# A transformer block on one core: V kept in DRAM as pairs of rows, and a newly searched order

## The chip, the core and the metric

The kernel runs on one core of a Trainium2 chip. A core has five engines that run their own instruction streams and meet through semaphores: PE (TensorE, the matrix multiplier), DVE (VectorE), ACT (ScalarE), POOL (GpSimd) and SP (SyncE), which here does nothing but issue transfers to the core's 16 DMA engines. The metric is device time in microseconds (us) for one execution; lower is better. The time before is the median of three runs, 244.95 us (243.38 to 245.19).

## What is computed

A block with adaptive layer norm on 2048 tokens of width 512: a dilated sliding-window attention with 32 heads of 16, then a gated feed-forward (FFN) of width 1792. Cut to what matters:

```python
mod = (silu(c) @ w_mod).reshape(...)          # sa, ca, ga, sb, cb, gb
h = layernorm(x) * (1 + ca) + sa
qkv = (h @ wqkv)                              # H = 32 heads, Dh = 16
W, dil = (8, 2)
idx = arange(S)[:, None] - arange(W)[None, :] * dil      # token s sees s, s-2, ..., s-14
logits = einsum('bhsd,bhswd->bhsw', q, k[idx]) * Dh ** -0.5    # idx < 0 is masked
o = einsum('bhsw,bhswd->bhsd', softmax(logits), v[idx])
x = x + ga * (o @ wo)
h = layernorm(x) * (1 + cb) + sb
x = x + gb * ((silu(h @ w1) * (h @ w3)) @ w2)
```

## The kernel before

The 2048 tokens are 16 tiles T of 128. Tensors are bfloat16; sums are kept in PSUM in float32, in 8 banks of 128 x 512.

**QKV.** Layer norm and projection run over four groups of four tiles. Q and K are kept transposed (channels on partitions). V is projected with tokens on partitions (`proj_v`, matmuls of L796), evicted by ACT (L806) into one of `NVB = 6` buffers `vb`, and stored to a DRAM scratch `v_dram`, one row of 512 channels (1 KB) per token, with 16 rows of zeros ahead of token 0 (written once from `zrow`). A buffer of `vb` is free again when its store has landed.

**Logits** (`logits`). For a tile, DVE multiplies q by the eight shifted views of k in one instruction (L827). PE sums over the 16 channels of each head by matmuls with the 0/1 matrix `E_sb` (L836): four column groups of the array run side by side, each for 32 of the tile's tokens. The result has 32 rows (heads) per group of 32 tokens; its columns are shift by token, the tokens in the order "even ones, then odd ones".

**Softmax** (`shift`, `exps`, `softmax`). DVE and ACT work on these columns, for two tiles at once; PE turns the result (L891), so that partitions are (token pair, shift) and the two tokens of a pair lie in the free dimension; ACT evicts it to `al` (L895).

**Values** (`values`). Four loads per tile, one for every 32 tokens, bring V from DRAM back to `vsh`: 128 pieces of 2 KB each. Partition (t, w) gets the two neighbouring rows 2t - 2w and 2t + 1 - 2w, so 16 pairs by 8 shifts. DVE multiplies by the weights in place (L911). PE sums over the eight shifts with a 0/1 matrix `ind` (L920), ACT evicts (L926) into `oa`, and a DMA transpose turns that into `ot`, which is multiplied by `wo` (L944) and added to x by DVE (L948). There are three `vsh` buffers (one of them in the place of `wqkv`, once the projections are done) and two `oa`.

**FFN.** Six groups of two or four tiles (`FFN`): PE computes gate and up (L960), ACT and DVE make silu(gate) * up, PE multiplies by w2 (L1003, L991), DVE adds x and the result is stored. The weights come in four column slices each, `w1_0` to `w1_3`, `w3_0` to `w3_3`.

**Order.** The builder first makes about 1200 operations with what each reads and writes. A list `ORDER`, found ahead of time by a search over a cost model, gives the sequence; every engine runs its operations in that sequence and none overtakes another on its engine. A list `SLOTS` gives the buffer of each value. `PACKET` and the cost constants were used by the search alone and do nothing in the kernel as it runs. On PE the FFN matmuls of the first tiles are placed between the attention work of later tiles. All transfers but one go through SP's queue, issued by L124: weights, V stores, V loads, transposes and output stores stand there in one line, and where one of them has to wait for a semaphore, those behind it wait too. The words "58th on SP" below count positions in this line from zero.

Of the kernel before, what the change touches and what calls it, by code (L numbers as in the profile page):

```python
# [256 lines left out]
def c_act(n):  # L257
    return 66 + n * 107 // 128
# [8 lines left out]
PACKET = {T: 95 if T < 2 else 122 for T in range(16)}  # L267
# [7 lines left out]
AVCOL = frozenset(range(16))  # L275
# [5 lines left out]
def _build(p, A_x, A_wqkv, A_wo, B_w1, B_w3, B_w2, c, w_mod, out):  # L281
# [34 lines left out]
    ind = sb([P, 2, 16, 2], bf, "ind")  # L316
    before = sb([P, W, 2, 16], bf, "before")
# [25 lines left out]
    zrow = at([PAD, D], bf, "zrow", 25600)  # L343
# [54 lines left out]
    p.op("pool", lambda e: e.memset(ind[:], 0.0), 100, k, w=[vind])  # L398
    for r in range(2):
        p.op("pool", lambda e, r=r: e.memset(ind[:, r, :, r], 1.0), 100, k, w=[vind])  # L400
    for edge, mult in ((0, 1), (W - 1, -1)):
        p.op("pool", lambda e, edge=edge, mult=mult: e.affine_select(
            out=ind[:], in_=ind[:], compare_op=ALU.is_ge, fill=0.0, base=edge, pattern=[[0, 2], [-W * mult, 16], [0, 2]],
            channel_multiplier=mult), 250, k, w=[vind])
    p.op("pool", lambda e: e.memset(before[:], 0.0), 250, k, w=[vbefore])
    p.op("pool", lambda e: e.affine_select(out=before[:], in_=before[:], compare_op=ALU.is_ge, fill=BEFORE, base=0,
                                           pattern=[[-DIL, W], [1, 2], [2, 16]], channel_multiplier=0), 400, k, w=[vbefore])
# [36 lines left out]
    p.dma(v_dram[0:PAD, :], zrow[:], ("load", 11), (16, 1024), r=[vzrow] + wm_hold, w=[vvpad], store=True)  # L444
# [345 lines left out]
    def proj_v(T, tt, vh):  # L790
# [19 lines left out]
        p.dma(v_dram[PAD + T * P:PAD + (T + 1) * P, :], lambda: vt.at[:], k, (128, 1024), r=[vt], w=[vd], cost=400, store=True)  # L810
# [5 lines left out]
    def logits(Ts):  # L816

        vl = Val("ps_l", psum)
        for i, T in enumerate(Ts):
# [10 lines left out]
            def red(e, i=i, T=T, vp=vp):  # L830
                c0 = vl.at * 512 + i * W * 32
                if T == 0:
                    e.matmul(PALL[0:32, c0:c0 + W * 32], ones[:, 0:32], before[:], start=True, stop=False, tile_position=(0, 0))
                for ft in range(KT):
                    for q in range(4):
                        ins = e.matmul(PALL[32 * q:32 * q + 32, c0:c0 + W * 32], E_sb[:, ft, :], bass.AP(vp.at, ft * P + 32 * q, [[W * KT * P, P], [KT * P, W], [1, 2], [2, 16]]),  # L836
                                       start=(ft == 0 and (T > 0 or q > 0)), stop=(ft == KT - 1), tile_position=(0, 32 * q))
                return ins

            p.op("pe", red, C_RED + (110 if T == 0 else 0), ("lg", T), r=[vp, vE] + ([vbefore, vc] if T == 0 else []), part=[vl], tiled=True)  # L840
# [32 lines left out]
    def softmax(Ts, vl, ve, vx_):  # L873
# [12 lines left out]
        def turn(e):  # L886
            b = bank(vt).bitcast(bf)
            for i in range(n):
                at = b[:, i * 256:(i + 1) * 256].rearrange("p (q y h) -> p q y h", q=4, y=2)
                for y in range(2):  # L890
                    ins = e.transpose(at[:, :, y, :], bass.AP(ve.at[0], i * W * 32 + y * 16 * W, [[2 * W * 32, P], [1, P]]), ident[:])  # L891
            return ins
# [6 lines left out]
    def values(T, i, val):  # L899
# [3 lines left out]
        for q in range(4):  # L903
# [11 lines left out]
        if T in AVCOL:  # L915
            def acc(e):
                b = bank(vo)
                for r in range(2):
                    for q in range(4):
# [4 lines left out]
            p.op("pe", acc, C_RED, ("ac", T), r=[vv, vind], w=[vo], tiled=True)  # L924
            va = Val("oa", oapool)
            p.op("act", lambda e: e.activation(va.at[:], bank(vo), ACT.Copy), c_act(512), ("ac", T), r=[vo], w=[va])  # L926
            p.dma(lambda: vt.at[:], lambda: va.at[:], ("ac", T), (128, 1024), r=[va], w=[vt], cost=1250, transpose=True)
        else:
            def acc(e):
                b = bank(vo)  # L930
                for g in range(4):
                    for ft in range(KT):
                        for r in range(2):
                            ins = e.matmul(b[:, ft * P + 32 * g:ft * P + 32 * g + 32], vv.at[:, 2 * g + r, ft * P:(ft + 1) * P],
                                           ind[:, r].rearrange("p t r -> p (t r)"), start=(r == 0), stop=(r == 1))
                return ins

            p.op("pe", acc, C_ACC, ("ac", T), r=[vv, vind], w=[vo])
            p.op("act", lambda e: e.activation(vt.at[:].rearrange("p k t -> p (k t)"), bank(vo), ACT.Copy), c_act(512), ("ac", T), r=[vo], w=[vt])
# [224 lines left out]
```

## Time and profile before

| | |
|---|---|
| median of 3 runs | 244.95 us |
| the profiled execution, its own time | 245.03 us |
| its span, first to last instruction | 243.0 us |
| instructions | 4593 |
| granted TensorE clock | 1.00 throughout |
| issues of V loads | 64, of 256 KB each |
| issues of V stores | 16, of 128 KB each |

The profile is of one execution. Busy times are per engine; a busy PE is not PE at its peak, since ends of matmuls are modelled. "PEld" is the loading of the stationary operand, which runs beside the matmuls. In views of waits, "A <- B" is an instruction A that sat idle until B released it; L124 is the line of the helper that issues every DMA, so DMAs are told apart by their tiles.

### The profile page before, as it was taken

The page shows a single profiled execution, that of the slowest core. Times are in us where ns is not written, and L with a number is a line of the kernel's source. Part 1 is how long each engine was busy: PE and PEld are TensorE (multiplying, and loading weights), DVE is VectorE, ACT ScalarE, POOL GpSimd, SP SyncE. Part 2 cuts the span into 40 slices and gives each one's busy share as a digit, 9 for nine tenths or more (in the row PEclk, how much of TensorE's full clock was granted, in tenths as well). Part 3 has the DMA queues.
Part 4 walks back from the last instruction along what each step waited for, and adds up shares of the span by engine and source line. Part 5 has one row for each costly group of instructions (what it writes and reads, how often), then busy time and mean ns, then how long its engine had stood idle before and what let it go on. Part 6 is the DMA issues. An engine that isn't in the chain of part 4 may idle for free.

```text
span 243.0 us, 4593 instructions
## 1 busy us (share of the span) xinstructions
PE 232.6 (96%) x1789; PEld 134.1 (55%) x1814; DVE 169.1 (70%) x295; ACT 158.3 (65%) x324; POOL 23.0 (9%) x54
## 2 busy tenths in 40 slices
PE   7899999999789999999999999999999999999995
PEld 1665454545357885654444444444655447576874
DVE  5489999999697999999999698366133213155242
ACT  4358597799788978777967798876653674321300
POOL 6421330011001100011000040110000100000000
DMA  5999899599589999699897824884020030011002
GB/s 167 288 361 265 272 298 215 134 272 275 175 196 291 256 242 245 154 214 137 251 227 195 237 65 68 194 182 99 3 65 1 3 86 0 0 46 43 3 23 65
DMA packets 44685, 38.33 MB, mean 158 GB/s; under 512 B 19560, under 2 KB 35960, under 8 KB 44664
## 3 DMA queue, kind: packets, MB, share of 16 engines
q1 hardware_dynamic: 44656, 38.04, 62.6%
q8 instruction: 14, 0.23, 0.4%
q14 instruction: 7, 0.06, 0.1%
q10 hardware_dynamic: 8, 0.00, 0.0%
HBM read 29.62 MB, written 4.21 MB: 139 GB/s over the span
## 4 chain that ended last, share of the span: by engine, by line
PE 65%; DMA 14%; SPq 7%; ACT 6%; DVE 5%; issue 2%; POOL 1%; ACTq 0%
PE pall L960 33%; PE pall L1003 14%; SPq L124 7%; PE pall L777 5%; DMA sb_wm_g<-in_w_mod_dram 4%; DMA sb_ot<-sb_oa 4%; PE pall L944 3%; DMA v_scratch_dram<-sb_v 3%; PE pall L991 3%; PE pall L796 2%; PE pall L920 2%; DMA sb_h<-sb_xn 2%; PE pall L836 2%; ACT sb_h L653 2%; ACT sb_xn L620 1%
## 5 line engine op out<-in xcount | busy, mean ns | idle before, releaser
L960 PE MATMUL pall<-sb_h,sb_w 128*128 128x256 bf16 (+1 forms) x668 | 103.0, 308 | 1.4 <-DMA sb_w<-in_B_w_dram 0.7
L960 PEld LDWEIGHTS pall<-sb_h,sb_w 128*128 128x128 bf16 x672 | 64.4, 98 | 38.0 <-ACT sb_hh L970 1.5
L966 ACT ACTIVATE sb_sg<-pall 128x256 bf16<-128x256 f32 (+1 forms) x84 | 35.0, 453 | 33.5 <-PE pall L960 25.9
L1003 PE MATMUL pall<-sb_w,sb_hh 128*128 128x512 bf16 x187 | 43.2, 379 | 0.6
L827 DVE TENSOR_TENSOR sb_pq<-sb_q,sb_kT 128x4096 bf16<-128x4096 bf16 x16 | 36.3, 2277 | 0.0
L970 ACT ACTIVATE sb_hh<-pall 128x256 bf16<-128x256 f32 (+1 forms) x56 | 26.5, 494 | 10.3 <-PE pall L960 10.3
L1003 PEld LDWEIGHTS pall<-sb_w,sb_hh 128*128 128x128 bf16 x196 | 18.9, 98 | 21.3 <-DVE sb_hh L971 0.6
L974 DVE TENSOR_TENSOR sb_hh<-sb_sg,pall 128x256 bf16<-128x256 bf16 x28 | 11.1, 418 | 26.6 <-PE pall L960 23.3
L911 DVE TENSOR_TENSOR sb_vsh<-sb_vsh,sb_al 128x4096 bf16<-128x4096 bf16 x12 | 27.4, 2286 | 2.4 <-ACT sb_al L895 1.3
L777 PE MATMUL pall<-sb_h,sb_wqkv 128*128 128x512 bf16 x107 | 25.8, 379 | 1.2 <-ACT sb_v L806 0.9
L971 DVE TENSOR_TENSOR sb_hh<-sb_sg,sb_hh 128x256 bf16<-128x256 bf16 (+1 forms) x56 | 17.9, 349 | 7.3 <-ACT sb_sg L966 4.0
L1019 DVE TENSOR_TENSOR sb_o<-pall,sb_x 128x512 bf16<-128x512 f32 (+1 forms) x18 | 11.0, 627 | 13.4 <-PE pall L1003 7.3
L626 POOL TENSOR_SCALAR sb_rs<-sb_var 128x2 f32<-128x2 f32 x8 | 4.9, 608 | 145.5 <-ACT sb_xn L620 145.5
L777 PEld LDWEIGHTS pall<-sb_h,sb_wqkv 128*128 128x128 bf16 x112 | 10.3, 98 | 12.0 <-ACT sb_v L806 1.4
L944 PE MATMUL pall<-sb_wo,sb_ot 128*128 128x512 bf16 x60 | 15.7, 379 | 0.9 <-DMA sb_ot<-sb_oa 0.5
L796 PE MATMUL pall<-sb_wqkv,sb_h 128*128 128x512 bf16 x61 | 15.9, 379 | 0.3 <-issue 0.2
L653 ACT ACTIVATE sb_h<-sb_h,sb_modc 128x512 bf16<-128x512 bf16 (+1 forms) x20 | 13.2, 721 | 3.9 <-DMA sb_h<-sb_xn 3.9
L948 DVE SCALAR_TENSOR_TENSOR sb_x<-pall,sb_x 128x512 bf16<-128x512 f32 x16 | 10.9, 688 | 6.5 <-PE pall L944 6.5
L631 ACT ACTIVATE sb_xn<-sb_x,sb_nb,sb_rs 128x512 bf16<-128x512 bf16 x16 | 12.6, 808 | 4.1 <-DVE sb_nb L628 4.1
L620 ACT ACTIVATE sb_xn<-sb_x,sb_nm 128x512 bf16<-128x512 bf16 x16 | 11.5, 720 | 2.9 <-DVE sb_nm L616 2.7
L785 ACT ACTIVATE sb_q<-pall 128x512 bf16<-128x512 f32 x16 | 9.3, 604 | 4.4 <-PE pall L777 4.4
L594 DVE BATCH_NORM_STATS2 sb_st<-sb_x 128x6 f32<-128x512 bf16 x15 | 9.9, 676 | 2.7 <-DMA sb_x<-in_A_x_dram 2.7
(112 smaller groups left out, 236.1 us busy)
## 6 DMA issues: line engine op xcount, KB each, us to landing
sb_vsh<-v_scratch_dram SPq DMA_DIRECT2D x48, 256.0 KB, 4.9
sb_vshx<-v_scratch_dram SPq DMA_DIRECT2D x16, 256.0 KB, 4.0
sb_w<-in_B_w_dram SPq DMA_DIRECT2D x6, 512.0 KB, 7.8
sb_w<-in_B_w_dram SPq DMA_DIRECT2D x6, 384.0 KB, 4.4
v_scratch_dram<-sb_v SPq DMA_DIRECT2D x16, 128.0 KB, 4.3
out_dram<-sb_o SPq DMA_DIRECT2D x14, 128.0 KB, 2.0
sb_x<-in_A_x_dram SPq DMA_DIRECT2D x3, 512.0 KB, 9.8
sb_wqkv<-in_A_wqkv_dram SPq DMA_DIRECT2D x2, 512.0 KB, 7.9
```

Of the source, the lines that this page charges most:

```text
L124: return e.dma_start(a, b, transpose=True) if transpose else e.dma_start(a, b)
L653: return e.activation(vh.at[:, ft, 0:n * P], vh.at[:, ft, 0:n * P], ACT.Identity, bias=modc[:, 8 * which + ft:8 * which + ft + 1], scale=m ...
L777: ins = e.matmul(bank(vp)[:, 0:n], wqkv[:, t, kind * D + ft * P:kind * D + (ft + 1) * P], vh.at[:, t, 0:n], start=(t == ORDER[0]), stop=(t ...
L796: ins = e.matmul(bank(vp), vh.at[:, t, tt * P:(tt + 1) * P], wqkv[:, t, 2 * D:3 * D], start=(t == ORDER[0]), stop=(t == ORDER[-1]))
L827: return e.tensor_tensor(vp.at[:], in0, in1, ALU.mult)
L911: return e.tensor_tensor(v_w, v_w, a_w, ALU.mult)
L944: ins = e.matmul(bank(vy), vt.at[:, ft, :], wo[:, ft, :], start=(ft == 0), stop=(ft == KT - 1))
L960: ins = e.matmul(bank(vp)[:, 0:n], wt[:, t, fi * P:(fi + 1) * P], vh.at[:, t, 0:n], start=(t == 0), stop=(t == KT - 1))
L966: p.op("act", lambda e: e.activation(vt.at[:, 0:n], bank(vgp)[:, 0:n], ACT.Silu), c_act(n), k, r=[vgp], w=[vt], table="silu")
L970: p.op("act", lambda e: e.activation(vh_.at[:, 0:n], bank(vup)[:, 0:n], ACT.Copy), c_act(n), k, r=[vup], w=[vh_])
L971: p.op("dve", lambda e: e.tensor_tensor(vh_.at[:, 0:n], vt.at[:, 0:n], vh_.at[:, 0:n], ALU.mult), 60 + n * 69 // 128, k, r=[vt], w=[vh_], ...
L1003: ins = e.matmul(bank(vz), vhh[fi].at[:, tt * P:(tt + 1) * P], w2[:, fi, :], start=(fi == 0), stop=(fi == NF - 1))
```

## The change

`v_dram` now has one row of 2 KB per token: its first half holds V two tokens back, its second half V of the token itself. Every V row is therefore written twice: the store of a tile has 256 pieces of 1 KB instead of 128, from the same SBUF tile read twice. The zeros ahead are 18 rows of 2 KB, and the store of tile 0 overlaps them, so it waits until the zeros have landed.

A load still has 128 pieces of 2 KB, but partition (t, w) is now one token t of 32 and one of four double shifts w: its piece holds the rows t - 4w - 2 and t - 4w. There are still four loads per tile and eight rows of 512 in each partition of `vsh`. The tokens of the logits stand in their own order, so L836 reads its moving operand contiguously instead of in steps of two; the turn of the weights (L891) takes shift by token with a step of two instead of contiguous columns; `ind` is one matrix of 128 x 32 for both halves instead of two. The branch for tiles outside `AVCOL`, which no tile took, goes, and a branch for tiles in `EARLY`, which is empty, comes. Two POOL instructions that built `ind` go.

`ORDER` and `SLOTS` are replaced. The operations are the same ones otherwise, so the two sequences can be compared. On PE the first 47 operations, up to the keys of the first tiles, are the same. Positions on SP of what the prediction speaks of, read from the two lists (V_T: store of tile T; L_T: loads of tile T; ot_T: transpose of tile T):

| | before | after |
|---|---|---|
| zeros | 21 | 18 |
| V0, V1 | 22, 23 | 22, 23 |
| wmg1 (last columns of w_mod) | 17 | 21 |
| w1_0, w3_0 | 61, 69 | 19, 59 |
| L0, L1 | 25 to 35 | 26 to 33 |
| V9, V8 | 58, 59 | 44, 61 |
| V5, V7 | 47, 50 | 58, 53 |
| L2, L3 | 44 to 57 | 45 to 55 |
| w1_1, w3_1 | 49, 60 | 56, 47 |
| first of L5 | 62 | 62 |
| ot_2, ot_3 | 63, 65 | 60, 64 |

Buffers of `vb`: before, V12 and V15 take the buffers of V9 and V8, and are evicted 76th and 81st on ACT. After, V15, V14 and V13 take those of V7, V5 and V8, and are evicted 85th, 84th and 89th. On PE the first FFN matmul stands at 157 in both; before it uses w1_1 and the next w3_1, w1_0, w1_2; after, the first eight use w1_1, w1_0 and w3_1 and w3_0.

```diff
+WL = 4
+TB = W // DIL
+EARLY = frozenset(())
...
-    ind = sb([P, 2, 16, 2], bf, "ind")
-    before = sb([P, W, 2, 16], bf, "before")
+    ind = sb([P, P // WL], bf, "ind")
...
-    v_dram = nc.dram_tensor("v_scratch_dram", (PAD + S, D), bf)
+    v_dram = nc.dram_tensor("v_scratch_dram", (PAD + S + DIL, 2 * D), bf)
...
-    p.dma(v_dram[0:PAD, :], zrow[:], ("load", 11), (16, 1024), r=[vzrow] + wm_hold, w=[vvpad], store=True)
+    p.dma(bass.AP(v_dram, 0, [[2 * D, PAD + DIL], [D, 2], [1, D]]), bass.AP(zrow, 0, [[D, PAD + DIL], [0, 2], [1, D]]), ("load", 11), (36, 1024), r=[vzrow] + wm_hold, w=[vvpad], store=True)
...
-        p.dma(v_dram[PAD + T * P:PAD + (T + 1) * P, :], lambda: vt.at[:], k, (128, 1024), r=[vt], w=[vd], cost=400, store=True)
+        p.dma(bass.AP(v_dram, (PAD + T * P) * 2 * D + D, [[2 * D, P], [3 * D, 2], [1, D]]), lambda: bass.AP(vt.at, 0, [[D, P], [0, 2], [1, D]]), k,
+              (256, 1024), r=[vt] + ([vvpad] if T == 0 else []), w=[vd], cost=400, store=True)
...
-                        ins = e.matmul(PALL[32 * q:32 * q + 32, c0:c0 + W * 32], E_sb[:, ft, :], bass.AP(vp.at, ft * P + 32 * q, [[W * KT * P, P], [KT * P, W], [1, 2], [2, 16]]),
-                                       start=(ft == 0 and (T > 0 or q > 0)), stop=(ft == KT - 1), tile_position=(0, 32 * q))
+                        cols = [q, [TB, 32]] if T in EARLY else [32 * q, [1, 32]]
+                        ins = e.matmul(PALL[32 * q:32 * q + 32, c0:c0 + W * 32], E_sb[:, ft, :],
+                                       bass.AP(vp.at, ft * P + cols[0], [[W * KT * P, P], [KT * P, W]] + cols[1:]),
+                                       start=(ft == 0 and (T > 0 or q >= NBEF)), stop=(ft == KT - 1), tile_position=(0, 32 * q))
...
-                    ins = e.transpose(at[:, :, y, :], bass.AP(ve.at[0], i * W * 32 + y * 16 * W, [[2 * W * 32, P], [1, P]]), ident[:])
+                    ins = e.transpose(at[:, :, 1 - y, :], bass.AP(ve.at[0], i * W * 32 + y, [[2 * W * 32, P], [2, P]]), ident[:])
...
-                  bass.AP(v_dram, (PAD + T * P + 32 * q) * D, [[2 * D, 16], [-DIL * D, W], [1, 2 * D]]), ("vl", T), (128, 2048),
-                  r=[vv_dram[T]] + ([vv_dram[T - 1]] if T else [vvpad]), part=[vv], group=loads, cost=640, again=PACKET[T])
+                  bass.AP(v_dram, row + 32 * q * 2 * D, [[2 * D, P // WL], [-DIL * 4 * D, WL], [1, 2 * D]]), ("vl", T), (P, 2048),
+                  r=near, part=[vv], group=loads, cost=640, again=PACKET[T])
...
-                        ins = e.matmul(b[32 * q:32 * q + 32, :], ind[:, r].rearrange("p t r -> p (t r)"), vv.at[:, 2 * q + r, :], start=(r == 0),
-                                       stop=(r == 1), tile_position=(0, 32 * q))
+                    ins = e.matmul(b[32 * q:32 * q + 32, :], ind[:], vv.at[:, 2 * q + r, :], start=(r == 0), stop=(r == 1),
+                                   tile_position=(0, 32 * q))
...
 ORDER = [
...
 SLOTS = [
...
```

In it `row = 2 * D * (PAD + T * P)`, and `near` is the list of stores that the load waited for before: the tile's own and the one ahead of it, or the zeros.

More of the change, by code (lines that the diff above doesn't have):

```diff
@@ L266 @@
 BLOCKS = [[[0, 1]], [[2, 3]], [[4, 5]], [[6, 7]], [[8, 9]], [[10, 11]], [[12, 13], [14, 15]]]
-PACKET = {T: 95 if T < 2 else 122 for T in range(16)}
+WL = 4
+TB = W // DIL
+EARLY = frozenset(())
+PACKET = {T: 352 if T in EARLY else 92 for T in range(16)}
 WMOD = 66
@@ L342, in _build @@
     wm_s = [at([P, KT, 1024], bf, f"wm_s{i}", 12288 * i) for i in range(2)]
-    zrow = at([PAD, D], bf, "zrow", 25600)
+    zrow = at([PAD + DIL, D], bf, "zrow", 25600)
     thc, c4, c4s = at([KT, P], f32, "thc", 24576), at([KT, P], bf, "c4", 25088), at([KT, P], bf, "c4s", 25344)
@@ L831, in red @@
                 c0 = vl.at * 512 + i * W * 32
[L832 to L833 removed]
+                for q in range(NBEF if T == 0 else 0):
+                    e.matmul(PALL[32 * q:32 * q + 32, c0:c0 + W * 32], ones[:, 0:32], before[:, q], start=True, stop=False,
+                             tile_position=(0, 32 * q))
                 for ft in range(KT):
                     for q in range(4):
[L836 to L840 removed]
+                        cols = [q, [TB, 32]] if T in EARLY else [32 * q, [1, 32]]
+                        ins = e.matmul(PALL[32 * q:32 * q + 32, c0:c0 + W * 32], E_sb[:, ft, :],
+                                       bass.AP(vp.at, ft * P + cols[0], [[W * KT * P, P], [KT * P, W]] + cols[1:]),
+                                       start=(ft == 0 and (T > 0 or q >= NBEF)), stop=(ft == KT - 1), tile_position=(0, 32 * q))
+                return ins
+            o = p.op("pe", red, C_RED + (110 if T == 0 else 0), ("lg", T), r=[vp, vE] + ([vbefore, vc] if T == 0 else []), part=[vl], tiled=True)
+            if T == 0 and NBEF > 1:
+                late["w2_0"].deps[o] = False
         return vl
@@ L902, in values @@
         loads = []
-        for q in range(4):
+        near = [vv_dram[T]] + ([vv_dram[T - 1]] if T else [vvpad])
+        row = 2 * D * (PAD + T * P)
+        early = T in EARLY
+        if early:
+            p.dma(lambda: vv.at[:], bass.AP(v_dram, row, [[TB * 2 * D, P // WL], [-DIL * 4 * D, WL], [1, TB * 2 * D]]), ("vl", T),
+                  (P, 2048), r=near, w=[vv], cost=640, again=PACKET[T])
+        for q in range(0 if early else 4):
             p.dma(lambda q=q: vv.at[:, 2 * q:2 * q + 2, :],
-                  bass.AP(v_dram, (PAD + T * P + 32 * q) * D, [[2 * D, 16], [-DIL * D, W], [1, 2 * D]]), ("vl", T), (128, 2048),
-                  r=[vv_dram[T]] + ([vv_dram[T - 1]] if T else [vvpad]), part=[vv], group=loads, cost=640, again=PACKET[T])
+                  bass.AP(v_dram, row + 32 * q * 2 * D, [[2 * D, P // WL], [-DIL * 4 * D, WL], [1, 2 * D]]), ("vl", T), (P, 2048),
+                  r=near, part=[vv], group=loads, cost=640, again=PACKET[T])
         def av(e):
@@ new lines, in acc @@
+        def acc(e):
+            b = bank(vo)
+            for r in range(2):
+                for q in range(4):
+                    ins = e.matmul(b[32 * q:32 * q + 32, :], ind[:], vv.at[:, 2 * q + r, :], start=(r == 0), stop=(r == 1),
+                                   tile_position=(0, 32 * q))
+            return ins
+        p.op("pe", acc, C_RED, ("ac", T), r=[vv, vind], w=[vo], tiled=True)
+        va = Val("oa", oapool)
+        p.op("act", lambda e: e.activation(va.at[:], bank(vo), ACT.Copy), c_act(512), ("ac", T), r=[vo], w=[va])
@@ new lines, in values, with turn @@
+        if early:
+            vq = Val("ps_oT", psum)
+            def turn(e):
+                b = bank(vq).bitcast(bf)
+                for ft in range(KT):
+                    ins = e.transpose(b[:, ft * P:(ft + 1) * P], va.at[:, ft * P:(ft + 1) * P], ident[:])
+                return ins
+            p.op("pe", turn, 228, ("ot", T), r=[va, vident], w=[vq])
+            p.op("act", lambda e: e.activation(vt.at[:].rearrange("p k (t q) -> p k t q", q=TB),
+                                               bank(vq).bitcast(bf)[:, 0:KT * P].rearrange("p (k q t) -> p k t q", k=KT, q=TB), ACT.Copy),
+                 c_act(512), ("ot", T), r=[vq], w=[vt])
+        else:
+            p.dma(lambda: vt.at[:], lambda: va.at[:], ("ac", T), (128, 1024), r=[va], w=[vt], cost=1250, transpose=True)
```

38 lines of the change are left out of this document (10 added, 28 removed), and 128 rows, old and new, of tables (ORDER, SLOTS).

## The prediction

> **What bounds the kernel now.** I read the page first, then the stretches by time, the chain, the waits, and SP's own line.
>
> ```profile
> PE 232.6 (96%) x1789; PEld 134.1 (55%) x1814; DVE 169.1 (70%) x295; ACT 158.3 (65%) x324; POOL 23.0 (9%) x54
> PE   7899999999789999999999999999999999999995
> DVE  5489999999697999999999698366133213155242
> DMA  5999899599589999699897824884020030011002
> ```
>
> PE is busy for 232.6 of 243.0 us and its matmuls are the same after the change, so what can be won lies in its 10.4 us of idle time. A slice is 6.1 us. PE dips at the start and in slices 10 and 11 (61 to 73 us); DVE is nearly full from slice 4 on and dips with PE there; the DMA engines are full for most of the first 130 us. Windows of 6 us place it:
>
> ```profile
> 12.00:18.00 6.00, 5.90 (x50) 3.69 (x50) 5.18 (x19) 3.15 (x6) 1.10 (x3) 1.00 1.08 360
> 18.00:24.00 6.00, 5.41 (x72) 3.20 (x71) 5.60 (x9) 5.06 (x9) 0.83 (x2) 1.00 1.04 276
> 54.00:60.00 6.00, 5.95 (x37) 3.12 (x37) 6.00 (x9) 5.96 (x12) 1.33 (x2) 1.00 1.07 266
> 60.00:66.00 6.00, 4.72 (x59) 2.04 (x60) 4.18 (x3) 3.89 (x9) 0.00 (x0) 1.00 0.64 214
> 66.00:72.00 6.00, 5.16 (x45) 3.14 (x43) 5.92 (x6) 5.59 (x11) 0.00 (x0) 1.00 0.70 167
> 72.00:78.00 6.00, 5.64 (x51) 4.55 (x49) 4.52 (x11) 4.58 (x14) 0.07 (x1) 1.00 1.04 291
> 84.00:88.00 4.00, 4.00 (x40) 3.58 (x37) 4.00 (x6) 3.18 (x10) 0.00 (x0) 1.00 1.14 227
> 88.00:93.00 5.00, 4.95 (x40) 3.10 (x40) 5.00 (x10) 4.50 (x11) 0.00 (x0) 1.00 1.07 246
> 240.00:243.00 3.00, 0.23 (x3) 0.00 (x0) 0.68 (x2) 0.00 (x0) 0.00 (x0) 1.00 0.15 44
> ```
>
> The second time in a row is PE's busy time, the last three numbers the granted clock, the DMA share and GB/s. From 60 to 78 us PE loses 18 - (4.72 + 5.16 + 5.64) = 2.48 us, from 18 to 24 us 0.59, and 2.77 at the very end, where the last sum is added and stored. DVE loses 18 - (4.18 + 5.92 + 4.52) = 3.38 us between 60 and 78, so it is not what PE waits for there. The chain and the waits say what is:
>
> ```profile
> 54.39 7.94 DMA v_scratch_dram<-sb_v
> ...
> 62.41 0.60 ACT sb_v L806
> ...
> 68.27 5.52 DMA sb_ot<-sb_oa
> ...
> 73.84 1.04 PE pall L944 x4
> ```
>
> ```profile
> ACT sb_v L806 <- DMA v_scratch_dram<-sb_v: 2.1, 1, 2.1
> PE pall L777 <- ACT sb_v L806: 0.9, 1, 0.9
> PE pall L960 <- DMA sb_w<-in_B_w_dram: 0.7, 1, 0.7
> PE pall L944 <- DMA sb_ot<-sb_oa: 0.4, 1, 0.4
> ```
>
> ```profile
> 54.39 1.79 SPq L124 DMA_DIRECT2D v_scratch_dram<-sb_v  x2
> 56.22 1.15 SPq L124 DMA_DIRECT2D sb_w<-in_B_w_dram  x2
> 65.18 0.52 SPq L124 DMA_DIRECT2D sb_vsh<-v_scratch_dram  x1
> 66.38 1.22 SPq L124 DMA_TRANSPOSE sb_ot<-sb_oa  x1
> ...
> 68.27 1.19 SPq L124 DMA_TRANSPOSE sb_ot<-sb_oa  x1
> 69.51 1.88 SPq L124 DMA_DIRECT2D sb_vsh<-v_scratch_dram  x3
> ```
>
> Three things, all of them transfers. V9's store, issued at 54.39, lands 7.94 us later behind the loads of tiles 2 and 3; V12, which needs its buffer, sits on ACT for 2.1 us, with everything behind it on ACT. SP itself stands from 57.4 to 65.18 at the first load of tile 5, whose buffer is not free, and the transpose of tile 2 stands behind it. Then w3_0, 69th on SP, and the transpose of tile 3 are late for PE.
>
> **V loads.** Count, size and pieces stay (64 of 256 KB); only the addresses change. In 84 to 93 us little but loads of tiles 6 and 7 runs: the DMA engines are as full (1.14 and 1.07) as with weights in 12 to 18 us (1.08), and move 227 to 246 GB/s instead of 360. So a load takes 262 KB / 237 = 1.11 us and would take 0.73 us at the weights' rate. Before, each 2 KB pair is read eight times for a group of 32 tokens, from 23 pairs; after, each 2 KB row at most four times, from 44 rows. If the repeats are what slows them, part of the 0.38 us comes back; if not, nothing does. A loss I bound by the slower of the two windows (262 / 227 = 1.15 us, +0.04). I take half, 0.19 us per load, 0.75 per tile, as no row tells the two apart. The Trainium skill (DMA: Bandwidth & Descriptors, section Bandwidth, its measured table) speaks against a gain: there the rate follows the size of the transfer, 138 GB/s at 64 KB and 341 at 1 MB, which would leave these loads where they are; the rows above fit that as well, since the weights come in larger transfers, and by it the sum in the queue below would be +4.5 us instead of +1.5.
>
> **V stores.** Each is 128 KB longer.
>
> ```profile
> v_scratch_dram<-sb_v SPq DMA_DIRECT2D x16, 128.0 KB, 4.3
> out_dram<-sb_o SPq DMA_DIRECT2D x14, 128.0 KB, 2.0
> out_dram<-sb_o SPq DMA_DIRECT2D x4, 64.0 KB, 1.5
> v_scratch_dram<-sb_zrow SPq DMA_DIRECT2D x1, 16.0 KB, 6.6
> ```
>
> 131 KB more at 360 or 227 GB/s is 0.36 or 0.58 us of all engines; I take 0.45. (For one store alone the output rows give 2.0 - 1.5 = 0.5 us per 64 KB, so about 1 us later to land on a quiet queue; the 4.3 us here is mostly queue.)
>
> **The sum in the queue.** Up to the loads of tile 3 there are ten stores and 16 loads: 10 x 0.45 = 4.5 us more against 16 x 0.19 = 3.0 less. So where PE waits, the layout by itself lengthens the queue by 1.5 us. Later, 48 loads give back 9.1 us against 6 x 0.45 = 2.7, but in 84 to 93 us PE is already busy for 8.95 of 9: that gain is covered, and worth nothing to the end of the program. The layout alone is then no gain; what counts is the order.
>
> **The order.** After, the buffers of V9 and V8 are no longer wanted at once: V14, V15 and V13 wait for V5, V7 and V8 (58th, 53rd and 61st on SP) and are evicted 84th to 89th on ACT instead of 76th and 81st. Some eight evictions of about 0.6 us (the row above: 0.60) are 4.8 us more room, against 1.5 us of longer queue. The transpose of tile 2 (60th) now stands ahead of the first load of tile 5 (62nd), so that load's wait for its buffer no longer holds it. And w3_0 is 59th instead of 69th, with w1_1, w1_0 and w3_1 ahead of it, and the first FFN units use just these. So all three causes go, and I take off the whole 2.48 us. What is late next is V13, whose buffer comes with V8's store, which is behind the transpose of tile 2; it costs nothing as long as that store lands before ACT's 89th.
>
> **The start.** The first 47 operations of PE are the same. Behind them:
>
> ```profile
> 17.61 1.41 SPq L124 DMA_DIRECT2D sb_wo<-in_A_wo_dram  x1
> 19.07 0.59 SPq L124 DMA_DIRECT2D v_scratch_dram<-sb_zrow  x1
> 20.34 4.04 SPq L124 DMA_DIRECT2D v_scratch_dram<-sb_v  x2
> ```
>
> ```profile
> PE pall L555 <- DMA sb_wm_g<-in_w_mod_dram: 0.3, 1, 0.3
> PE pall L833 <- DVE sb_pq L827: 0.3, 1, 0.3
> ```
>
> The first logits (L833) move from 90th to 107th on PE, so their 0.3 us goes; the wait for wmg0 stays. The new wait is V0's store on the zeros: they land 6.6 us after issue and are now three issues earlier, about 4 us at 1.41 us each (SP is held up by a full queue there), so at about 15 + 6.6 = 21.7 us, against 20.34 for V0's issue before. SP stands for 0 to 1.4 us; behind it are V1, two pieces of wo and the loads of tiles 0 and 1. I take 0: w1_0 and wmg1 are queued ahead and keep the engines moving, and SP waited for V1 there anyway (two stores over 4.04 us). Without that cover it is +1.4.
>
> **PE's own work.** L836 read in steps of two and now reads contiguously; L891's weights go the other way.
>
> ```profile
> L836 PE MATMUL pall<-sb_pq,sb_E 128*32 128x256 bf16 x256 | 8.9, 271 | 0.0
> L891 PEld LDWEIGHTS pall<-sb_ident,sb_attn 128*128 128x128 bf16 x32 | 2.5, 98 | 1.5
> L991 PE MATMUL pall<-sb_w,sb_hh 128*128 128x256 bf16 x56 | 6.3, 272 | 0.0
> ```
>
> With steps of two a matmul of 256 columns took 271 ns, with a contiguous operand 272 (L991): no gain in L836. No row has a weight load in steps of two; if it doubled, 32 x 98 ns = 3.1 us would be added beside matmuls, of PEld's 55%; below, zero. I take 0, by L836. Two POOL instructions less, on an engine with 9%: 0.
>
> **Sum.** 245.03 us for the profiled execution (243.0 of span and 2.0 around it), less 2.48 and 0.3: 242.2. The median, 244.95, is 0.08 lower; I leave that out. A measurement of this kernel can tell about 1%, 2.45 us, from no change: below 242.5 is faster, above 247.4 slower.
>
> **Rivals.** *The gap moves.* DVE is as full as PE before the gap (6.00 of 6 in 54 to 60), and a search that frees one place puts its lateness in another: V13, or the loads of tile 5, or the weights of the third slice. For it: the queue at that place is no shorter, by my own sum. Against it: DVE had 3.38 us to spare. With half of the gap left the time is 245.0 - 1.3 = 243.7, with all of it and the 1.4 us of the zeros 246.4; the case spans 242.6 to 247.
>
> *The stores decide, slower.* If the loads gain nothing, the queue up to tile 3 is 4.5 us longer. V8's store then lands after V13 wants its buffer, the transposes and the weights of the FFN come behind the same queue, and PE, which has used up its projections by then, waits. The order takes off at most about 1 us of that (SP no longer held at tile 5): 245.0 + 4.5 - 1.0 = 248.5. For it: the queue is full there (1.07 in 54 to 60), and the loss lies at the only place where PE has nothing else. Against it: those 4.8 us of room. It decides if a load stays above about 1.0 us; at 1.11 - 4.5 / 16 = 0.83 the stores are paid for. The rule of the Trainium skill named above would give this case too.
>
> ```profile
> PE pall L539 <- DVE sb_ones L383: 1.5, 1, 1.5
> ```
>
> **Chances.** Forecast 0.44, the gap moves 0.30, the stores 0.26. Faster by over 1%: 0.43; within 1%: 0.31; slower: 0.26, each case lying almost wholly on its side. Low end: all idle time but the first 1.5 us, before the first matmul, and the last 2.77 is 10.4 - 4.3 = 6.1, which gives 238.9 and is not reached; with the gap, the start's 0.59 and half of the other 3.0 gone it is 240.4, and I say 240.0. The high end takes in the stores at 248.5. For the forecast alone I would say 240.5 to 242.5.
>
> **What would show it.** Windows from 60 to 78 us with PE at 5.9 or more, and no wait of L806 on a V store: the order's step is right. A V-load stretch with full engines near 290 GB/s: the half is right; at 240: the rival's rate; at 360: I undersold it. Landing of V stores well over 4.3 us with PE idle behind it: the stores decide. SP held at V0 past 22 us, with loads of tile 1 late for DVE: the zeros. L891's weight loads over 98 ns: the bound I set to zero. I am wrong altogether if PE's idle time grows at a place where no transfer is late.

## The result, and the profile after

The changed kernel takes 243.4 us (median of 20 runs, 242.36 to 247.04) against 244.99 us for the kernel before (20 runs): a ratio of 0.9954, with a 95% interval from 0.9934 to 0.9974. Medians here are of all runs, while ratios and their intervals are of the fast runs alone, so a ratio is not the quotient of the two medians (0.9935 here). A second comparison gave 244.15 us and 0.9957 (0.9926 to 0.9989). By the ratio it is faster by about 0.45%, 1.1 us: the direction was forecast, and about two fifths of the size (2.8 us). The profiled execution took 244.1 us, with a span of 242.1.

The page of the changed kernel, engines and slices (a slice is 6.05 us):

```profile
PE 233.8 (97%) x1814; PEld 134.3 (55%) x1814; DVE 169.7 (70%) x295; ACT 157.3 (65%) x324; POOL 19.5 (8%) x52
PE   7799999999989998999999999999999999999995
DMA  6999699999899799895590974722030002001002
```

The dip of PE in slices 10 and 11 is nearly gone, and a smaller one has come in slice 15. Windows of the changed kernel (PE's busy time is the second time in a row; the last three numbers are clock, DMA share and GB/s):

```profile
18.00:24.00 6.00, 5.72 (x64) 3.74 (x62) 5.80 (x18) 4.57 (x9) 2.78 (x6) 1.00 1.12 265
54.00:60.00 6.00, 6.00 (x38) 3.10 (x37) 5.98 (x9) 6.00 (x13) 0.92 (x2) 1.00 1.04 365
60.00:66.00 6.00, 6.00 (x69) 2.88 (x68) 5.96 (x6) 5.96 (x13) 0.00 (x0) 1.00 0.88 288
66.00:72.00 6.00, 5.29 (x41) 3.73 (x39) 5.97 (x6) 5.44 (x13) 0.00 (x0) 1.00 1.12 194
72.00:78.00 6.00, 5.83 (x78) 4.42 (x79) 4.82 (x12) 3.97 (x11) 1.00 (x2) 1.00 1.07 355
84.00:90.00 6.00, 5.87 (x69) 3.93 (x68) 5.17 (x8) 4.88 (x14) 0.00 (x0) 1.00 0.95 261
90.00:96.00 6.00, 4.86 (x37) 2.64 (x36) 5.58 (x8) 2.90 (x6) 0.00 (x0) 1.00 1.10 293
```

From 60 to 78 us PE now loses 0.71 + 0.17 = 0.88 us instead of 2.48. From 84 to 96 it loses 0.13 + 1.14 = 1.27, where it lost 0.05 before. So 1.60 us were won at the place that the prediction spoke of, and 1.22 lost at a later one. A second profiled execution of the changed kernel (after_again) loses 1.15 us in 60 to 78 and 1.72 in 84 to 96: the picture is the same, the sizes move by some tenths. (Some matmul records can be missing from a trace, 25 of 1814 in the kernel before and none in the first one of the changed kernel; differences of 0.05 us in a window mean nothing.) The chain and the waits name the later one (start, length, what):

```profile
66.95 5.08 DMA sb_ot<-sb_oa
...
86.33 5.96 DMA sb_ot<-sb_oa
...
92.33 1.04 PE pall L960 x4
```

```profile
PE pall L960 <- DMA sb_ot<-sb_oa: 2.2, 3, 1.1
...
ACT sb_v L809 <- DMA v_scratch_dram<-sb_v: 0.7, 1, 0.7
```

The output product of tile 4 (L960, which was L944) stands until the transpose of its input has landed, 5.96 us after issue. SP's line shows what is ahead of that transpose:

```profile
79.81 5.11 SPq L124 DMA_DIRECT2D sb_vsh<-v_scratch_dram  x7
84.96 0.60 SPq L124 DMA_DIRECT2D sb_w<-in_B_w_dram  x1
86.33 1.21 SPq L124 DMA_TRANSPOSE sb_ot<-sb_oa  x1
```

Seven V loads and a piece of w2: the same kind of lateness as before, at another transfer. The loads alone don't explain it, since eight of them stand ahead of this transpose in the kernel before, too:

```profile
81.74 5.94 SPq L124 DMA_DIRECT2D sb_vsh<-v_scratch_dram  x8
91.39 1.21 SPq L124 DMA_TRANSPOSE sb_ot<-sb_oa  x1
```

```profile
99.08 0.81 PE pall L944 x3
```

There it is issued at 91.39, 3.7 us behind the last of the loads, and PE comes to its product at 99.08 (the last row, from the chain), 7.7 us after the issue. In the changed kernel it is issued at 86.33, 1.4 us behind the last load, and PE is ready for it at 91.2, 4.9 us after the issue. What one V transfer takes from issue to landing has changed too (the page's list of DMA issues; the kernel before had 4.3 us for the stores, with half the bytes, and 4.9 for the loads):

```profile
sb_vsh<-v_scratch_dram SPq DMA_DIRECT2D x48, 256.0 KB, 4.3
...
v_scratch_dram<-sb_v SPq DMA_DIRECT2D x16, 256.0 KB, 3.8
```

Stores of twice the size land sooner than before; with the old order on the new layout, in the two runs below, their medians are 4.2 and 4.4 us. Neither is the longer queue of the prediction's sum.

### The profile page after: what moved, and what is told of

Its sections match the earlier page's. It is cut to its first block, busy times and chain, and to the rows that moved or that the text cites. A ratio compares the mean times of both kernels' runs of the same rounds, so it can differ in the third digit from the quotient of the medians.

```text
span 242.1 us, 4621 instructions
## 1 busy us (share of the span) xinstructions
PE 233.8 (97%) x1814; PEld 134.3 (55%) x1814; DVE 169.7 (70%) x295; ACT 157.3 (65%) x324; POOL 19.5 (8%) x52
## 4 chain that ended last, share of the span: by engine, by line
PE 84%; DMA 9%; SPq 3%; ACT 2%; issue 1%; DVE 0%
PE pall L976 37%; PE pall L1019 17%; PE pall L780 10%; DMA sb_ot<-sb_oa 6%; PE pall L960 6%; PE pall L799 3%; SPq L124 3%; PE pall L842 3%; DMA sb_wm_s<-in_w_mod_dram 3%; PE pall L1007 3%; PE pall L934 2%; PE pall L671 1%; PE pall L900 1%; PE pall L744 1%; ACT sb_h L679 1%
## 5 line engine op out<-in xcount | busy, mean ns | idle before, releaser
L982 ACT ACTIVATE sb_sg<-pall 128x256 bf16<-128x256 f32 (+1 forms) x84 | 36.6, 461 | 32.4 <-PE pall L976 27.9
L1019 PE MATMUL pall<-sb_w,sb_hh 128*128 128x512 bf16 x196 | 44.6, 379 | 0.0
L780 PE MATMUL pall<-sb_h,sb_wqkv 128*128 128x512 bf16 x112 | 26.9, 379 | 0.0
L960 PE MATMUL pall<-sb_wo,sb_ot 128*128 128x512 bf16 x64 | 16.1, 379 | 2.2 <-DMA sb_ot<-sb_oa 2.2
L629 POOL TENSOR_SCALAR sb_rs<-sb_var 128x2 f32<-128x2 f32 x8 | 2.0, 254 | 156.6 <-ACT sb_xn L623 156.6
L940 ACT ACTIVATE sb_oa<-pall 128x512 bf16<-128x512 f32 x16 | 9.7, 612 | 4.4 <-PE pall L934 4.3
```

The costliest lines, as they stand in the source:

```text
L780: ins = e.matmul(bank(vp)[:, 0:n], wqkv[:, t, kind * D + ft * P:kind * D + (ft + 1) * P], vh.at[:, t, 0:n], start=(t == ORDER[0]), stop=(t ...
L960: ins = e.matmul(bank(vy), vt.at[:, ft, :], wo[:, ft, :], start=(ft == 0), stop=(ft == KT - 1))
L982: p.op("act", lambda e: e.activation(vt.at[:, 0:n], bank(vgp)[:, 0:n], ACT.Silu), c_act(n), k, r=[vgp], w=[vt], table="silu")
L1019: ins = e.matmul(bank(vz), vhh[fi].at[:, tt * P:(tt + 1) * P], w2[:, fi, :], start=(fi == 0), stop=(fi == NF - 1))
```

## The experiments

All ratios are to the kernel before, measured on the same chip beside the run. There were three sets: four runs (the kernel before at 245.38 us there), four runs (245.28), two runs (245.07).

### The layout without the order: layout_only

```diff
 (all of the change, except:)
-ORDER = [...]   # the new searched order
+ORDER = [...]   # that of the kernel before, operation by operation; SLOTS likewise
```

> The new layout of V (its stores, loads and masks) under the old order and the old buffers. Theory A (the order brings the gain, the layout only shifts DMA work to and fro): the packets of the V loads take about 100 ns as in the changed kernel instead of 126, the stores twice their bytes, and the time stays within 1 us of before, 244 to 246 us; the wait of V12's eviction on V9's store shrinks but the transposes and w3_0 are still late, so PE still loses 1.5 us or more from 60 to 78 us. Theory B (the faster loads themselves empty the queue where PE waits): most of the gain is here already, 243.5 us or less, and PE loses under 1 us from 60 to 78. Theory C (the doubled stores hurt): above 246.5 us.

Measured: 243.85 us (12 runs), ratio 0.9925 (0.9894 to 0.9956). The layout by itself is faster, by about 1.8 us, as theory B had it. Its windows:

```profile
54.00:60.00 6.00, 5.95 (x37) 3.05 (x37) 6.00 (x9) 5.97 (x13) 1.34 (x2) 1.00 1.06 389
60.00:66.00 6.00, 6.00 (x74) 3.20 (x72) 5.55 (x5) 5.58 (x12) 0.00 (x0) 1.00 0.62 216
66.00:72.00 6.00, 5.38 (x43) 3.84 (x42) 6.00 (x7) 5.21 (x13) 0.00 (x0) 1.00 0.84 213
72.00:78.00 6.00, 5.94 (x59) 4.47 (x58) 4.91 (x11) 5.53 (x18) 1.78 (x2) 1.00 0.98 300
```

In 54 to 60 us the DMA engines are as full as before (1.06 against 1.07) and move 389 GB/s instead of 266. PE's idle time from 60 to 78 us falls from 2.48 to 0.68 us with the old order; what is left is mostly one wait for FFN weights (0.6 us). The stores of V9 and V8, the two that are issued between 54 and 57 us, carry it. From issue to landing they took in the kernel before:

```profile
DMA to landing us min/median/max: 7.6/7.7/7.9
```

and in layout_only:

```profile
who waited for it (us, times):
  ACT sb_v L809: 0.4, 1
...
DMA to landing us min/median/max: 6.0/6.2/6.3
```

V12's wait for that buffer shrinks from 2.1 to 0.4 us. So the old order was late because the loads in its queue were slow; with faster loads it is nearly in time.

### The order without the layout: order_only

```diff
 (the kernel before, except:)
-ORDER = [...]   # the old order
+ORDER = [...]   # the new searched order; SLOTS likewise
```

> The old layout (pairs of neighbouring rows, single stores) under the new order and the new buffers. Theory A (the order brings the gain): 243 to 244 us, about as the changed kernel. Theory B (the new order needs the faster loads): 245.5 us or more, with V-load packets at about 126 ns and PE waiting for transposes or weights between 66 and 110 us, where the changed kernel hardly waits.

Measured: 248.01 us (6 runs), ratio 1.0128 (1.0079 to 1.0178). The order, put on the old layout, costs 3.1 us. Waits of its profiled execution (which took 250.57 us, so they are on the long side):

```profile
PE pall L920 <- DVE sb_vsh L911: 3.3, 2, 2.4
PE pall L944 <- DMA sb_ot<-sb_oa: 2.4, 2, 1.4
```

```profile
84.00:90.00 6.00, 4.95 (x45) 3.50 (x44) 4.90 (x4) 4.59 (x13) 0.00 (x0) 1.00 1.09 245
90.00:96.00 6.00, 3.55 (x43) 2.23 (x41) 4.61 (x6) 2.18 (x6) 0.00 (x0) 0.91 1.14 238
```

The sums over V (L920) wait for products that wait for loads, and the output products for transposes, most of all in 84 to 96 us, the place that is also late in the changed kernel. (The granted clock is 0.91 in the second window, so not all of that loss need be the order's.) The new order relies on the loads' speed and has no use of its own where the loads are slow.

### The price of the stores: double_store

```diff
-    v_dram = nc.dram_tensor("v_scratch_dram", (PAD + S, D), bf)
+    v_dram = nc.dram_tensor("v_scratch_dram", (2 * (PAD + S), D), bf)
...
-        p.dma(v_dram[PAD + T * P:PAD + (T + 1) * P, :], lambda: vt.at[:], k, (128, 1024), r=[vt], w=[vd], cost=400, store=True)
+        p.dma(bass.AP(v_dram, (PAD + T * P) * D, [[D, P], [(PAD + S) * D, 2], [1, D]]), lambda: bass.AP(vt.at, 0, [[D, P], [0, 2], [1, D]]), k, (256, 1024), r=[vt], w=[vd], cost=400, store=True)
```

> The kernel before, with every V tile stored a second time to rows that nothing reads (256 pieces of 1 KB per store, as in the changed kernel); loads and order as before. My price of the stores in the queue: 0.45 to 0.54 us of all DMA engines each, 4.5 to 5.4 us up to the loads of tile 3. If the queue up to there decides, the wait of V12's eviction grows by 3 to 5 us and the time is 248 to 250 us. If the stores are mostly covered, 245 to 246.5 us.

Measured: 246.5 us (12 runs), ratio 1.0057 (1.0023 to 1.0091): 1.4 us slower. The stores are mostly covered: sixteen doubled ones cost the end of the program 1.4 us, where the prediction's sum gave ten of them 4.5 us of the queue.

### Two output products later on PE: wo_late

The order of the changed kernel, with two output products moved on PE behind work that was ready (names of the planner's operations: wo3 is the output product of tile 3, at4 the turn of the weights of tile 4, f16 an FFN unit, ac6 the sum over V of tile 6):

```diff
-wo3
 at4
 f2 gate
 f2 up
+wo3
...
-wo4
 f16 up
 ac6
 f17 up
+wo4
```

> The changed kernel with two products with wo moved later on PE: that of tile 3 by three places (behind the turn of tiles 4 and 5 and both halves of FFN unit 2), that of tile 4 by three (behind one FFN half, the sum of tile 6 and another FFN half). These are where PE waits for transposes, 0.7 us near 71 us and 1.1 us near 91 us. Theory A (these two waits are what the forecast missed): both vanish and the time falls by 1.0 to 1.8 us, to about 242 us. Rival (PE is handed the same lateness elsewhere, by DVE, which is full there): within 0.5 us of the changed kernel, 243.0 to 243.8 us.

Measured: 244.64 us (12 runs), ratio 0.9971 (0.9938 to 1.0004); the changed kernel had 0.9954. There is no gain, against theory A; the median lies even above the range of the rival. wo4 no longer waits at 91 us, and the time is lost beside it (windows and waits of its profiled execution, which took 245.94 us):

```profile
72.00:78.00 6.00, 5.08 (x64) 3.56 (x64) 4.57 (x7) 3.50 (x11) 0.09 (x1) 1.00 1.00 307
...
90.00:96.00 6.00, 4.73 (x45) 2.80 (x38) 4.76 (x6) 3.38 (x8) 0.00 (x0) 1.00 1.15 259
```

```profile
PEld pall L934 <- DVE sb_vsh L926: 1.5, 3, 0.9
PE pall L934 <- DVE sb_vsh L926: 0.6, 1, 0.6
PE pall L960 <- DMA sb_ot<-sb_oa: 0.3, 1, 0.3
```

The wait on the transpose falls from 2.2 to 0.3 us and one on the products of V takes its place. At 90 us this order is short of V itself, not only of one transpose.

### The two orders on the new layout: layout_again and after_again

These are layout_only and the changed kernel once more, unedited, on one chip.

> The layout of the change under the order of the kernel before, once more, beside the changed kernel on the same chip. Theory (the layout brings the whole gain, by emptying the queue before the store of V9; the new order brings nothing that can be told): the time lies within 0.5 us of the changed kernel's, at 243.4 to 244.2 us, PE over 6.0 us in 60-66 and its idle time in 60-78 at 0.5 to 1.0 us. Rival (the order brings a gain of its own once the loads are fast): the changed kernel is at least 0.6 us faster than this one. Second rival (the order costs): this one is at least 0.6 us faster.

> The changed kernel itself, on the same chip as the three others: 243.2 to 244.2 us by both theories; it is the mark for them.

Measured: layout_again 243.33 us (6 runs), ratio 0.9928 (0.9900 to 0.9955); after_again 244.15 us (12 runs), ratio 0.9957 (0.9926 to 0.9989). The medians on this chip are 0.82 us apart, which is the case of the second rival (the order costs). Over all sets, the old order stands twice at 0.993 and the new one at 0.9954 and 0.9957. The intervals overlap, so a cost of the new order of about 0.7 us is likely and not shown; a gain shows in neither pair. Windows of layout_again:

```profile
60.00:66.00 6.00, 6.00 (x72) 3.25 (x73) 5.61 (x5) 5.56 (x12) 0.00 (x0) 1.00 0.73 259
66.00:72.00 6.00, 5.31 (x44) 3.39 (x38) 5.95 (x6) 5.34 (x11) 0.00 (x0) 1.00 0.76 183
72.00:78.00 6.00, 6.00 (x54) 4.78 (x51) 4.66 (x11) 5.36 (x17) 0.85 (x1) 1.00 0.91 272
84.00:90.00 6.00, 6.00 (x61) 4.90 (x58) 6.00 (x11) 4.82 (x16) 0.00 (x0) 1.00 0.89 317
90.00:96.00 6.00, 5.95 (x41) 3.15 (x34) 6.00 (x9) 5.47 (x10) 0.00 (x0) 1.00 0.51 129
```

PE loses 0.69 us in 60 to 78 and 0.05 in 84 to 96, against 0.88 and 1.27 in the changed kernel: the loss at 91 us belongs to the new order.

### The zeros: layout_zeros_free and zeros_free

The same edit on the layout with the old order, and on the changed kernel:

```diff
-    p.dma(bass.AP(v_dram, 0, [[2 * D, PAD + DIL], [D, 2], [1, D]]), bass.AP(zrow, 0, [[D, PAD + DIL], [0, 2], [1, D]]), ("load", 11), (36, 1024), r=[vzrow] + wm_hold, w=[vvpad], store=True)
+    p.dma(bass.AP(v_dram, D, [[2 * D, PAD], [3 * D, 2], [1, D]]), bass.AP(zrow, 0, [[D, PAD], [0, 2], [1, D]]), ("load", 11), (32, 1024), r=[vzrow] + wm_hold, w=[vvpad], store=True)
...
-              (256, 1024), r=[vt] + ([vvpad] if T == 0 else []), w=[vd], cost=400, store=True)
+              (256, 1024), r=[vt], w=[vd], cost=400, store=True)
```

> The kernel of the run layout_again, with the zeros written only to the places that no store of V touches, so that the store of V0 doesn't wait for them. In that layout with the old order V0's store stood 3.4 us behind the zeros and PE lost 0.6 us before 30 us. Theory (that wait is on the path of this order): 0.4 to 0.7 us less than layout_again, 243.0 to 243.5 us, V0's store issued before 22 us and PE at 5.8 us or more in 24-30. Rival (what V0 waits for is made up later, or the loss before 30 us comes from the head's weights): within 0.3 us of layout_again, PE in 24-30 at 5.3 to 5.5 us again or the lost time back in a later window.

> The changed kernel with the zeros written only to the places that no store of V touches, so that the store of V0 doesn't wait for them. In the changed kernel V0's store waits 3.9 us for the zeros on SP, but PE works 6.0 of 6.0 us in the windows behind it. Theory (the wait lies beside other work): within 0.3 us of after_again, with V0's store issued before 19 us. Rival (the wait pushes every later transfer of the queue back, to the place at 91 us where PE stands for 1.1 us): 0.6 us or more faster than after_again and no wait over 0.5 us at 91 us.

Measured: layout_zeros_free 243.38 us (6 runs), ratio 0.9921 (0.9895 to 0.9946), beside 243.33 of layout_again. zeros_free 243.79 us (12 runs), ratio 0.9949 (0.9922 to 0.9976), beside 244.15 of after_again. Neither differs by what can be told. With the old order the wait was on the path for a while. A window of layout_again:

```profile
24.00:30.00 6.00, 4.39 (x38) 1.89 (x36) 6.00 (x15) 2.45 (x6) 1.85 (x4) 1.00 0.54 166
```

and the same window of layout_zeros_free:

```profile
24.00:30.00 6.00, 5.82 (x51) 2.81 (x49) 6.00 (x15) 3.42 (x8) 1.85 (x4) 1.00 0.79 247
```

V0's store goes out at 21.15 us instead of 24.25, and PE wins 1.43 us in this window; the two spans differ by 0.5 us (242.0 and 241.5) and the medians not at all. Part of the 1.43 is chance: layout_only, the same kernel as layout_again, has PE at 5.33 in this window, and the kernel before at 5.92. DVE is full at 6.00 in both windows, which may be why; that was not tried by itself. In zeros_free V0's store left at 21.50 us, not before 19 as expected, since the eviction of V0 itself starts only at 20.88; in the changed kernel it starts at 20.09 and the store goes at 22.25.

### Why the loads were slow: no_repeat and wide_repeat

Both are the kernel before with other addresses for the loads from tile 2 on (and a dependency on one earlier store); the sums over V are then of other rows.

```diff
 (no_repeat)
-                  bass.AP(v_dram, (PAD + T * P + 32 * q) * D, [[2 * D, 16], [-DIL * D, W], [1, 2 * D]]), ("vl", T), (128, 2048),
+                  bass.AP(v_dram, (PAD + T * P + 32 * q) * D, [[2 * D, 16], [-DIL * D, W], [1, 2 * D]]) if T < 2 else bass.AP(v_dram, (PAD + T * P + 32 * q - 224) * D, [[2 * D, P], [1, 2 * D]]), ("vl", T), (128, 2048),
...
 (wide_repeat)
+                  bass.AP(v_dram, (PAD + T * P + 32 * q) * D, [[2 * D, 16], [-DIL * D, W], [1, 2 * D]]) if T < 2 else bass.AP(v_dram, (PAD + T * P + 32 * q - 120) * D, [[10 * D, 16], [-10 * D, W], [1, 2 * D]]), ("vl", T), (128, 2048),
```

> The kernel before, in which each V load from tile 2 on reads 128 different pairs of rows, side by side over 256 rows, in place of 23 pairs that recur up to eight times; so other rows of V than the computation needs, the same number and size of transfers, and the stores as before. It asks why a load of 256 KB went at 224 to 246 GB/s before and over 300 GB/s with the new layout. Theory (the same rows are asked for again and again, and that is slow; the new layout recurs at most four times): the loads are as fast here as with the layout or faster, over 300 GB/s in 84-90, and the time is 242.5 to 244 us, with V9's store landing earlier and PE at 5.7 us or more in 60-66. Rival 1 (the time goes by the size of the transfer, 2 KB in all three): 220 to 250 GB/s in 84-90 and 245 us. Rival 2 (what is slow is a small stretch of memory, whatever recurs): fast here as well; the run wide_repeat tells it from the theory.

> The kernel before, in which each V load from tile 2 on reads 23 pairs of rows that recur up to eight times, as before, but with the pairs ten rows apart, over some 230 rows; so other rows of V than the computation needs, with the same number and size of transfers. Theory (recurring rows are slow): as slow as before, 220 to 250 GB/s in 84-90, and 244.5 to 246 us. Rival 1 (size alone): the same here, so no_repeat has to tell it. Rival 2 (a small stretch of memory is slow): over 300 GB/s in 84-90 and 242.5 to 244 us.

Measured: no_repeat 242.39 us (9 runs), ratio 0.9897 (0.9866 to 0.9928); wide_repeat 244.87 us (10 runs), ratio 1.0012 (0.9964 to 1.0060). In 60 to 66 us, and in 84 to 88 us, where all bytes moved are loads of tiles 6 and 7, no_repeat has

```profile
60.00:66.00 6.00, 6.00 (x75) 3.21 (x74) 5.55 (x5) 5.79 (x13) 0.00 (x0) 1.00 0.48 160
...
84.00:88.00 4.00, 4.00 (x40) 3.58 (x38) 4.00 (x8) 2.88 (x10) 0.00 (x0) 1.00 1.05 406
```

layout_again, with V loads alone in this stretch too, has

```profile
84.00:88.00 4.00, 4.00 (x38) 3.41 (x36) 4.00 (x5) 3.08 (x10) 0.00 (x0) 1.00 1.00 356
```

In wide_repeat and in the kernel before, other transfers still run beside these loads in 84 to 88 us (46% and 16% of the bytes). From 88 to 93 us all bytes are V loads in both: the kernel before has 1.07 and 246 GB/s there, and wide_repeat has

```profile
60.00:66.00 6.00, 4.86 (x32) 2.15 (x33) 5.29 (x4) 4.03 (x9) 0.00 (x0) 1.00 0.81 260
...
88.00:93.00 5.00, 4.95 (x47) 3.72 (x46) 5.00 (x8) 3.73 (x12) 0.00 (x0) 1.00 1.08 246
```

Number, size and pieces are the same in all four. Different rows go at 406 GB/s, rows that recur up to eight times at 246 whether they lie side by side or ten rows apart, and rows that recur at most four times at 356 (370 in layout_only; 298 in layout_zeros_free, with the engines at 0.90). The records of single packets say the same: the mean of all 2 KB pieces of the V loads is 128 ns in the kernel before, 128 in wide_repeat, 103 in no_repeat, and 98 to 100 in the two runs of the layout with the old order. So it is the addresses that made the loads slow, and neither size nor a small stretch of memory; recurrence fits all four. The rows of no_repeat are also contiguous as a whole; but those of the new layout recur and are not, and go as fast by their pieces. One thing stays open: both of the costlier patterns walk the source as 16 by 8 pieces, the two cheaper ones as 32 by 4 and as 128: no run has 16 by 8 pieces without recurrence, so the shape of the walk is not excluded as the cause.

## Why the prediction was right or wrong

**What bounds the kernel.** Right. Transfers late behind slow loads, V9's store among them, were the cause of the gap at 61 to 73 us: with faster loads, and nothing of the order touched, the gap closed from 2.48 to 0.7 us. How it divides among the three transfers named was not tried one by one.

**V loads.** Right in kind, and a little undersold. Repeats were named as the possible cause, and no_repeat and wide_repeat bear it out, but for the shape of the walk. A saving of 0.19 us per load was taken; a load has 128 pieces on 16 engines, eight on each, and 28 ns less for each is 0.22 us. The rule of the Trainium skill (DMA: Bandwidth & Descriptors, section Bandwidth, its measured table) that the rate follows the size of the transfer would have left the loads as they were; here transfers of one size went at 246 to 406 GB/s, so by it alone this change could not be judged. (The table there is of transfers issued by GpSimd, and these loads are issued by SP.)

**V stores.** About right: 0.45 us of all engines was taken for the second half of a store. The 1 KB pieces of the changed kernel's trace take 55.1 us of all engines together, against 46.5 before, which is 8.6 / 16 = 0.54 us for each; in layout_only they take 50.9, which is 0.28. (Pieces of some other loads are of 1 KB too, so this is an estimate.)

**The sum in the queue.** This step failed. It set ten stores against 16 loads since the start and got a queue 1.5 us longer, so that "the layout alone is then no gain; what counts is the order". But a queue forgets what it has worked off. The kernel before has this window, which the prediction left out:

```profile
42.00:48.00 6.00, 5.84 (x97) 3.35 (x97) 6.00 (x5) 4.23 (x9) 0.00 (x0) 1.00 0.53 128
```

The DMA engines are half idle from 42 to 48 us, and from 48 to 50 as well (shares of 0.46 and 0.58 by the microsecond), so hardly anything issued before then can delay a store issued at 54.39. What stands ahead of V9's store is at most what was issued from 47.6 us on: seven V loads, two stores and two pieces of weights. At the prediction's own prices that is 7 x 0.19 = 1.3 us less for the loads against two or three times 0.45 more for the stores, 0.9 to 1.35: about even, and not 1.5 us longer. The measured prices are better. The 2 KB pieces of the first 16 loads take 120 ns before and 88 in layout_only, so a load saves 8 x 32 ns = 0.26 us, and at the 389 GB/s of its windows the second half of a store is 131 KB / 389 = 0.34 us. Seven times 0.26 less, 1.8 us, against two or three times 0.34 more, 0.7 to 1.0, is 0.8 to 1.1 us less. Measured, the median landing of V9's and V8's stores came down by 1.2 us (7.7 to 6.5, layout_again) and 1.5 (to 6.2, layout_only). So the right stretch takes the wrong sign away, and the measured prices over it give most of the size. What the whole layout is worth fits its two halves: 2.5 us won by loads without recurrence (no_repeat), 1.4 lost by doubled stores (double_store), 1.1 in sum, and 1.8 measured, with intervals of about 0.8 us on each.

**The order.** This is the term of the forecast that failed with it. The order was given the whole 2.48 us, and the one later lateness that was looked at, V13's buffer, was set at nothing; the transpose of tile 3 was counted among what goes, and that of tile 4 was not looked at. In the changed kernel 1.60 of the 2.48 us went, and 1.22 came back at 84 to 96 us. And by the runs it was not the order that won: the gain of the layout alone is at least that of the whole change, and the order alone costs 3.1 us. Of its causes, three went as argued (no store is waited for at 61 us, the transpose of tile 2 no longer stands behind a load that has no buffer, w3_0 is in time), but the layout had already taken most of the first. The transpose of tile 3 did not: PE waits 0.9 us for it at 72 us, more than the 0.4 before. The new lateness is the transpose of tile 4: the order brings PE to its product 4.9 us after the issue instead of 7.7, and close behind the loads the transpose takes 5.96 us instead of 4.1.

The direction was right for a reason that the prediction had priced at nothing, the layout; that much was luck.

**The start.** The logits' 0.3 us and the wait for the zeros were set to -0.3 and 0. V0's store did leave past 22 us, at 22.25, the mark set for trouble; zeros_free shows that it costs nothing that can be told. In 18 to 24 us PE lost 0.28 instead of 0.59, but 1.12 in the second profiled execution, so no gain can be read off there. With the old order V0's store waits for the zeros too, and in 24 to 30 us PE loses 0.67 us in layout_only and 1.61 in layout_again, against 0.08 before and 0.18 without that wait (layout_zeros_free); the medians show nothing of it. The first 47 operations of PE are the same in both kernels, and in 6 to 12 us PE's busy time lies anywhere from 4.42 to 5.96 us in the profiles of this study, so differences there are left aside.

**PE's own work.** Right at zero for these two: L842 (which was L836) and L900 (which was L891) in the changed kernel,

```profile
L842 PE MATMUL pall<-sb_pq,sb_E 128*32 128x256 bf16 x256 | 8.9, 274 | 0.0
L900 PEld LDWEIGHTS pall<-sb_ident,sb_attn 128*128 128x128 bf16 x32 | 2.4, 98 | 1.6 <-DVE sb_x L964 0.4
```

274 ns against 271, and 98 against 98 with columns in steps of two.

**Loads behind 84 us are covered.** Right. In layout_again the DMA engines are at 0.51 in 90 to 96 us, against 1.14 before, and PE, at 5.95 there in both, gains nothing.

**The rivals.** "The gap moves" came nearest: the median lies beside its 243.7 for half of the gap, and the time is within 1% of before, the class that was given 0.31. The gap did move, to 91 us, though none of the three transfers it named is the late one. Its reason, a queue no shorter, was the failed sum again. "The stores decide" was priced with slow loads, and they were not slow.

## What to carry to other kernels

Count what is in a queue from the last window in which the queue ran dry, not from the start of the program, before you set added transfers against saved ones. When a change has a data layout and a new schedule in it, run each alone: here the layout was worth 1.8 us, the schedule no gain on top of it and a loss of 3.1 us without it. And where the DMA engines are full at a lower rate than at another place of the same kernel, look at the addresses: a buffer that is read with overlapping windows may be worth storing twice.

## What was not expected of the hardware

Loads of equal number, size and pieces from DRAM went at 246 GB/s when each 2 KB was asked for up to eight times within one load, and at 356 to 406 GB/s when it was asked for at most four times or once; up to four times cost nothing that shows (98 to 100 ns a piece against 103). The distance between the rows made no difference (128 ns a piece side by side and ten rows apart). Where between four and eight it begins was not tried, and neither were pieces in the slow shape, 16 by 8, that don't recur.
